# Identity products ahead of eight TensorE steps in a fused attention and two-MoE kernel

## The chip, the cores and the metric

The kernel runs on one core of one Trainium2 chip. The time is device microseconds (us) of one execution, as the median of several. Engines are named as in the profile: PE (TensorE matmul), PEld (TensorE weight load), DVE (VectorE), ACT (ScalarE), POOL (GpSimd), SP (SyncE, which issues nearly all DMAs).

## What is computed

A gated linear attention over 4 batches, 8 heads, 768 positions and head size 48; its output, as 3072 rows of 384, goes through a first MoE layer (384 to 2048 to 384, with a rational activation) and a second one (384 to 1536 to 384, gated by silu).

```python
def _attn_ref(q, k, v, alpha):
    ...
    for t in range(S):
        state = alpha[:, :, t, :, None] * state + np.einsum('bhd,bhe->bhde', k[:, :, t], v[:, :, t])
        y[:, :, t] = np.einsum('bhd,bhde->bhe', q[:, :, t], state)
def _moe_ref(x, w_in, w_out, a, b):
    h = x @ w_in
    P = a[0] + a[1] * h + a[2] * h * h + a[3] * h * h * h
    Q = 1.0 + np.abs(b[0]) * np.abs(h) + np.abs(b[1]) * h * h
    return (P / (Q + 1e-06)) @ w_out
def _moe2_ref(x, w_gate, w_val, w_out):
    g = x @ w_gate
    return (g / (1.0 + np.exp(-g)) * (x @ w_val)) @ w_out
```

## The kernel before

The attention is cut into 24 chunks of 128 positions (six to a batch). For a chunk, TensorE transposes alpha, k and q (`tr`, line 770, tiles aT, kT, qT), makes the scores (`scores`, line 821, sc), transposes the scaled k back (`back`, line 846, kn_ps), and in `values` makes the update of the state (line 865, upd), the chunk's own part of the output (line 870, yT) and the part from the state before it (line 876, yT). Between them DVE runs the two scans of the decay (lines 786 and 794, bb and cc) and scales k and q (lines 802 and 812, kt and qt), ACT copies results out of PSUM (779 al, 830 aa, 849 kn, 885 yo), and POOL masks the scores (835) and decays the state (904). The loads of a chunk are line 729 on SP's queue, into buffers that are used again: a load waits until TensorE has read the buffer. At the same time the MoE weights are split into two parts on DVE, POOL and ACT (`split_`; line 669 writes a scratch tile in a PSUM bank and line 675 reads it), and the first MoE's products (`mm1` and `mm2`, lines 955 to 957, tiles h and acc) begin as soon as 512 positions are there. The second MoE follows.

All operations are first collected in a `Plan`; each has the engine alternatives, what it depends on and the buffers that it writes. Then the table `ORDER` (lines 20 to 190) gives the order in which they are issued, written out by hand: entry x stands for operation x >> 1. Each engine runs its own operations in that order and never out of it. `Plan.order` also gives out the eight PSUM banks: the operation that opens a bank buffer takes the bank that has been free longest, and the bank goes back when the last operation on that buffer has been issued. The tile framework then adds the semaphore waits. A writer of a bank waits for the last reader of the buffer that had the bank before.

Before the attention, `keep_warm` (line 562) issues 9 products of a 128x128 identity with itself, and 20 more after the first chunk's qT; both go to bank 7, which nothing else uses at that time.

The eight operations that the change names, in the order in which TensorE reaches them (the bank is the one that the fills write, and its last reader is what `order` gives out for this table):

| operation | what it is | bank | last reader of that bank before |
|---|---|---|---|
| 90 | `tr`, aT | 5 | ACT, line 830 (aa) |
| 79 | `values` (bank of yT) | 1 | DVE, line 902 (st_c) |
| 146 | `tr`, aT | 4 | ACT, line 779 (al) |
| 135 | `values` (bank of yT) | 4 | DVE, line 675 (wout_x) |
| 161 | `values`, last chunk of a batch (yT) | 1 | DVE, line 902 (st_c) |
| 185 | `values` (bank of yT) | 4 | ACT, line 885 (yo) |
| 281 | `tr`, kT | 7 | DVE, line 902 (st_c) |
| 942 | `mm2` (bank of acc0) | 6 | DVE, line 675 (win_x) |

In `values` the products of upd come first and write another bank than yT.

Of the kernel before, what the change touches and what calls it, by code (L numbers as in the profile page):

```python
# [226 lines left out]
class Plan:  # L227
# [47 lines left out]

    def order(self, table):

        free = {c: list(range(k)) for c, k in self.classes.items()}
        todo = {}
        done = set()  # L280
        for x in table:
            i, k = x >> 1, x & 1
            _, how, deps, writes, follows = self.ops[i]
            assert i not in done and done.issuperset(deps) and done.issuperset(follows)
            done.add(i)
            for b in writes:
                if b.kind and b.ops[0] == i:
                    b.unit = free[b.cls].pop(0)
                    for j in set(b.ops):
                        todo.setdefault(j, []).append(b)  # L290
                    b.open = len(set(b.ops))
            for b in todo.get(i, ()):
                b.open -= 1
                if not b.open:
                    free[b.cls].append(b.unit)
            yield i, how[k][2]
        assert len(done) == len(self.ops)
# [160 lines left out]
def gla_moe_moe2_kernel(  # L458
# [15 lines left out]
    nc = tc.nc  # L474
# [23 lines left out]
    plan = Plan()  # L498
# [51 lines left out]
    ident = const.tile([128, 128], F32, name="ident")  # L550
# [792 lines left out]
        moe2(row, n, f0, f1, load_y(row[0], n), wg, wv, wo)  # L1343
    flag = bounds(end_a + 70.0, vs2[-1][0] - 70.0, vs2[-1][0] + 20.0)

    for x, (i, f) in enumerate(plan.order(ORDER)):
        if x == len(ORDER) - 18:
            tc.mark_branch_hint_location(
                "usual", "LikelyTaken", [mybir.EngineType.PE, mybir.EngineType.DVE, mybir.EngineType.SP])
        for b in plan.ops[i][3]:  # L1350
            if b.t is None:
                b.t = b.make()
        f()
    pb2.__exit__(None, None, None)
    pb.__exit__(None, None, None)
# [38 lines left out]
```

## Time and profile before

| | us |
|---|---|
| median of 3 runs | 989.08 |
| lowest, highest | 988.86, 990.64 |
| the profiled execution | 987.1 |
| its span, first to last instruction | 985.3 |

| engine | busy us | share | instructions |
|---|---|---|---|
| PE | 969.0 | 98% | 5355 |
| PEld | 805.6 | 82% | 5355 |
| DVE | 786.9 | 80% | 1493 |
| ACT | 588.9 | 60% | 1078 |
| POOL | 450.5 | 46% | 426 |

How to read it: the shares are means over stages that differ. In the table of 40 slices each digit is the busy share of one slice of 24.6 us in tenths, so the first four digits are the first tenth, in which attention, weight splitting and the first MoE overlap. A PE product is recorded with a modelled end, some 0.27 us after its start, while the next one can start 0.11 us after it; an idle time of PE is counted from that modelled end.

### The profile page before, as it was taken

What the parts mean: (1) busy time and instruction counts of PE and PEld (TensorE: products, weight loads), DVE (VectorE), ACT (ScalarE), POOL (GpSimd) and SP (SyncE); (2) the same over time, 40 slices, a digit from 0 to 9 for tenths busy, and PEclk for the clock granted to TensorE, in tenths of its full rate; (3) what the DMA queues carried; (4) which work ended last, traced back from release to release, by engine and by line L of the source; (5) the groups of instructions that cost most, each with busy time, mean ns of one, the idle gap of its engine ahead of it and who ended that gap; (6) DMA issues with size and microseconds to landing.
All of it is one profiled execution on the core that took longest, in us unless ns stands there. A gap on an engine that the chain in (4) does not pass through costs nothing.

```text
span 985.3 us, 15291 instructions
## 1 busy us (share of the span) xinstructions
PE 969.0 (98%) x5355; PEld 805.6 (82%) x5355; DVE 786.9 (80%) x1493; ACT 588.9 (60%) x1078; POOL 450.5 (46%) x426
## 2 busy tenths in 40 slices
PE   8899999999999999999999999999999999999997
PEld 7777888888888888888888888888888888888886
DVE  7999999999889888888898896799887767733222
ACT  4588998899999787789988675222122222212111
POOL 3368888799877676777987555000000000000000
PEclk9999999999999999999999999999999999999999
DMA  8978666531223242101221663346665545501000
GB/s 184 208 186 220 150 156 152 157 103 37 57 88 94 54 140 70 55 25 53 91 86 45 218 188 127 113 129 196 176 179 187 165 140 150 161 1 33 1 0 34
DMA packets 167137, 113.51 MB, mean 115 GB/s; under 512 B 115472, under 2 KB 140560, under 8 KB 167056
## 3 DMA queue, kind: packets, MB, share of 16 engines
q1 hardware_dynamic: 166768, 112.10, 40.7%
q8 instruction: 43, 0.70, 0.3%
q10 hardware_dynamic: 288, 0.39, 0.1%
q14 instruction: 38, 0.31, 0.1%
HBM read 95.95 MB, written 16.52 MB: 114 GB/s over the span
## 4 chain that ended last, share of the span: by engine, by line
PE 84%; DVE 8%; ACT 4%; issue 2%; POOL 1%; DMA 1%; SPq 0%; DVEq 0%; ACTq 0%; POOLq 0%
PE acc L955 6%; PE acc L956 6%; PE acc L957 6%; PE h L955 5%; PE h L957 5%; PE h L956 5%; PE pg L957 5%; PE pg L955 5%; PE pg L956 5%; PE pv L957 5%; PE pv L955 5%; PE pv L956 5%; PE po L955 4%; PE po L957 4%; PE po L956 4%
## 5 line engine op out<-in xcount | busy, mean ns | idle before, releaser
L925 POOL TENSOR_TENSOR gg<-t,gg 128x512 fp32r<-128x512 f32 x96 | 129.8, 1352 | 52.2 <-ACT gg L1014 50.9
L998 POOL TENSOR_TENSOR t<-t,t 128x512 f32<-128x512 f32 x96 | 127.7, 1332 | 29.2 <-ACT t L988 20.6
L1177 DVE TENSOR_TENSOR sg<-sg,pv 128x512 f32<-128x512 f32 (+1 forms) x73 | 49.4, 678 | 101.3 <-PE pv L957 101.0
L1179 ACT CAST pp<-sg 128x512 fp32r<-128x512 f32 (+1 forms) x73 | 44.8, 615 | 142.1 <-DVE sg L1177 126.7
L1175 ACT ACTIVATE sg<-pg 128x512 f32<-128x512 f32 (+1 forms) x73 | 43.0, 591 | 144.0 <-PE pg L957 143.8
L955 PE MATMUL h<-xt,win 128*128 128x512 f32 x288 | 114.4, 397 | 0.2 <-DVE wo_x L675 0.2
L955 PE MATMUL acc<-gg,wout 128*128 128x512 f32 x288 | 113.9, 396 | 0.5 <-DVE win_x L675 0.5
L957 PE MATMUL h<-xt,win 128*128 128x512 f32 x288 | 112.4, 390 | 0.0
L957 PE MATMUL acc<-gg,wout 128*128 128x512 f32 x288 | 112.3, 390 | 0.0
L956 PE MATMUL acc<-gg,wout 128*128 128x512 f32 x288 | 112.3, 390 | 0.0
L956 PE MATMUL h<-xt,win 128*128 128x512 f32 x288 | 112.2, 390 | 0.0
L957 PE MATMUL pg<-yy,wg 128*128 128x512 f32 x216 | 84.2, 390 | 0.0
L956 PE MATMUL pg<-yy,wg 128*128 128x512 f32 x216 | 84.2, 390 | 0.0
L955 PE MATMUL pg<-yy,wg 128*128 128x512 f32 x216 | 84.1, 389 | 0.0
L957 PE MATMUL pv<-yy,wv 128*128 128x512 f32 x216 | 84.0, 389 | 0.0
L956 PE MATMUL pv<-yy,wv 128*128 128x512 f32 x216 | 84.0, 389 | 0.0
L955 PE MATMUL pv<-yy,wv 128*128 128x512 f32 x216 | 84.0, 389 | 0.0
L1004 DVE SCALAR_TENSOR_TENSOR t<-t,h 128x512 f32<-128x512 f32 x96 | 65.4, 682 | 19.2 <-ACT h L1003 18.7
L995 ACT ACTIVATE t<-h,prm 128x512 f32<-128x512 f32 x96 | 73.8, 775 | 7.1 <-POOL gg L925 6.7
L1102 DVE TENSOR_SCALAR_CACHE_REDUCE chk_x<-chk_e 128x384 f32<-128x384 uint32 x136 | 73.6, 549 | 2.7
L1002 ACT ACTIVATE t<-t,oneps 128x512 f32<-128x512 f32 x96 | 69.5, 724 | 9.3 <-POOL t L998 8.9
L999 DVE TENSOR_TENSOR t<-t,h 128x512 f32<-128x512 f32 x96 | 65.1, 680 | 10.2 <-ACT t L995 10.0
(154 smaller groups left out, 2472.8 us busy)
## 6 DMA issues: line engine op xcount, KB each, us to landing
chk<-in_moe_w_out_dram SPq DMA_DIRECT2D x28, 384.0 KB, 3.2
yr<-y1d SPq DMA_DIRECT2D x36, 256.0 KB, 2.9
xr<-xd SPq DMA_DIRECT2D x27, 256.0 KB, 3.4
y1d<-ys SPq DMA_DIRECT2D x27, 256.0 KB, 3.2
win_st<-in_moe_w_in_dram SPq DMA_DIRECT2D x16, 384.0 KB, 4.1
wout_st<-in_moe_w_out_dram SPq DMA_DIRECT2D x16, 384.0 KB, 3.9
chk<-in_moe_w_in_dram SPq DMA_DIRECT2D x16, 384.0 KB, 3.5
nata<-in_alpha_dram SPq DMA_DIRECT2D x24, 192.0 KB, 3.6
```

What stands on the lines that cost most here:

```text
L925: return lambda: eng.tensor_tensor(out_(), in0(), in1().bitcast(F32), ALU.subtract)
L955: nc.tensor.matmul(out_, wh, xh, start=start, stop=False)
L956: nc.tensor.matmul(out_, wh, xl, start=False, stop=False)
L957: nc.tensor.matmul(out_, wl, xh, start=False, stop=stop)
L995: plan.op(v, [act(T, lambda: nc.scalar.activation(t4(), h(), AF.Identity, scale=a3, bias=a2), 2, False)], (hb,), (b4,))
L998: plan.op(v, [pool(T, lambda: nc.gpsimd.tensor_tensor(t1(), t1(), t2(), ALU.mult))], (b1, b2), (b1,))
L999: plan.op(v, [dve(T, lambda: nc.vector.tensor_tensor(t4(), t4(), h(), ALU.mult))], (b4, hb), (b4,))
L1002: plan.op(v, [act(T, lambda: nc.scalar.activation(t2(), t1(), AF.Ln, bias=oneps), 1)], (b1,), (b2,))
L1004: plan.op(v, [dve(T, lambda: nc.vector.scalar_tensor_tensor(t1(), t1(), ONE_EPS, h(), ALU.add, ALU.mult))], (b1, hb), (b1,))
L1102: [(DVE, 0.5, lambda: nc.vector.tensor_scalar(dst(), src(), bound, 0.0, op_, ALU.add, accum_out=cnt.t[:, c : c + 1]))],
L1177: plan.op(v, [(DVE, 0.07 + 0.53 * d, lambda sg=sg, z=z: nc.vector.tensor_tensor(sg.t[:, z], sg.t[:, z], pv.t[:, z], ALU.mult))], (sg, pv), ...
L1179: plan.op(v, [(ACT, 0.1 + 0.43 * d, lambda sg=sg, pp=pp, z=z: nc.scalar.copy(pp.t[:, 0, z], sg.t[:, z]))], (sg,), (pp,))
```

## The change

Eight operations get a number of products ahead of them. Just before such an operation is issued, and after its buffers have been made, the kernel issues that many transposes of the identity (128x128, the same product as in `keep_warm`) into the first 128 columns of the first bank that the operation opens. The operation's own products then overwrite the bank. `ORDER` stays as it is. `self.free` only keeps a name for the lists of free banks; nothing reads it.

```diff
     def order(self, table):
 
-        free = {c: list(range(k)) for c, k in self.classes.items()}
+        free = self.free = {c: list(range(k)) for c, k in self.classes.items()}
...
+    fills = {
+        90: 4, 79: 5, 146: 4, 135: 10, 161: 5, 185: 5, 281: 3, 942: 3,
+    }
     for x, (i, f) in enumerate(plan.order(ORDER)):
...
         for b in plan.ops[i][3]:
             if b.t is None:
                 b.t = b.make()
+        for b in plan.ops[i][3]:
+            if b.cls == "bank" and b.ops[0] == i:
+                for _ in range(fills.pop(i, 0)):
+                    nc.tensor.transpose(b.t[:, 0:128], ident, ident)
         f()
```

## Rows read from the trace of the kernel before

**Rows 1.** The page: busy tenths and granted clock in 40 slices
```profile
DVE  7999999999889888888898896799887767733222
PEclk9999999999999999999999999999999999999999
```

**Rows 2.** Busy time by stretch: length, engines (x instructions), granted clock, DMA share, GB/s
```profile
5.00:98.50 93.50, 85.55 (x899) 72.41 (x898) 90.87 (x151) 66.56 (x145) 49.95 (x56) 1.00 0.87 204
98.50:980.00 881.50, 880.10 (x4445) 730.45 (x4443) 696.07 (x1343) 521.00 (x933) 397.22 (x354) 1.00 0.36 106
```

**Rows 3.** Waits of DVE, 10 to 145 us: total, times, longest
```profile
DVE bb L786 <- ACT bC L798: 0.5, 1, 0.5
DVE wout L645 <- POOL wout_x L702: 0.4, 1, 0.4
DVE wout_x L675 <- POOL wout L645: 0.2, 1, 0.2
```

**Rows 4.** PE timeline (start, duration, what, count, [idle before]): identity products, next step
```profile
1.43 2.18 PE L562 MATMUL warm<-ident 128*128 128x128 f32 x9 [1.43 <-POOL ident masks.py:199]
6.08 2.35 PE L562 MATMUL warm<-ident 128*128 128x128 f32 x20
8.26 0.60 PE L770 MATMUL aT<-ident,nata 128*112 128x128 f32 x4
```

**Rows 5.** PE timeline: the five steps 90, 79, 146, 161 and 185
```profile
17.86 0.62 PE L770 MATMUL aT<-ident,nata 128*112 128x128 f32 x4 [0.63 <-DMA nata<-in_alpha_dram]
24.83 0.58 PE L865 MATMUL upd<-natv,kn 128*64 128x48 f32 x15 [0.87 <-ACT st_s L909]
30.61 0.62 PE L770 MATMUL aT<-ident,nata 128*112 128x128 f32 x4 [0.70 <-ACT wout L680]
44.94 1.31 PE L870 MATMUL yT<-aa,natv 128*64 128x128 f32 x16 [0.82 <-DMA natv<-in_v_dram]
51.03 0.58 PE L865 MATMUL upd<-natv,kn 128*64 128x48 f32 x15 [0.78 <-ACT al L779]
```

**Rows 6.** ACT timeline: the last reader of step 90's bank
```profile
15.88 1.07 ACT L830 COPY aa<-sc 128x512 f32<-128x512 f32 x2 [2.20 <-PE sc L821]
```

**Rows 7.** DVE timeline, 37 to 38.5 us: the bank's last reader, then qt
```profile
37.25 0.56 DVE L675 SCALAR_TENSOR_TENSOR wout_x<-wout_st,wout_e 128x384 uint32<-128x384 uint32 x1
37.72 0.68 DVE L812 TENSOR_TENSOR qt<-qT,bb 112x512 f32<-112x512 f32 x1
```

**Rows 8.** PE timeline: step 135, and a qT transpose further on
```profile
38.51 0.58 PE L865 MATMUL upd<-natv,kn 128*64 128x48 f32 x15 [1.61 <-ACT kn L849]
49.21 0.60 PE L770 MATMUL qT<-ident,natq 128*112 128x128 f32 x4
```

**Rows 9.** DVE timeline, 73 to 75.5 us: last readers of banks 7 and 6
```profile
73.91 0.34 DVE L902 TENSOR_TENSOR st_c<-upd,st_c 112x192 f32<-112x192 f32 x1
74.91 0.53 DVE L675 SCALAR_TENSOR_TENSOR win_x<-win_st,win_e 128x384 uint32<-128x384 uint32 x1
```

**Rows 10.** PE timeline: steps 281 and 942, and the next two waits behind them
```profile
74.31 0.65 PE L770 MATMUL kT<-ident,natk 128*112 128x128 f32 x4 [0.49 <-DVE st_c L902]
75.49 0.50 PE L955 MATMUL acc<-gg,wout 128*128 128x512 f32 x1 [0.54 <-DVE win_x L675]
79.74 0.60 PE L770 MATMUL qT<-ident,natq 128*112 128x128 f32 x4
80.41 0.65 PE L770 MATMUL aT<-ident,nata 128*112 128x128 f32 x4
141.00 0.61 PE L865 MATMUL upd<-natv,kn 128*64 128x48 f32 x15 [0.41 <-DVE t L1010]
```

**Rows 11.** PE, ACT and DVE timelines: where a late PE meets the next engine
```profile
50.43 0.68 DVE L812 TENSOR_TENSOR qt<-qT,bb 112x512 f32<-112x512 f32 x1
58.99 0.60 PE L770 MATMUL aT<-ident,nata 128*112 128x128 f32 x4
59.68 0.59 ACT L779 COPY al<-aT 112x512 f32<-112x512 f32 x1
```

## Prediction

> **What bounds the kernel now.** I read the page's slices first: DVE is at nine tenths from the second slice to the ninth, and the granted clock is full in all 40 slices [rows 1]. Then the busy time by stretch. From 98.5 us to 980 us TensorE is busy for 880.1 of 881.5 us, so there it sets the pace. In the first tenth it is not so: from 5 to 98.5 us TensorE is busy for 85.55 of 93.5 us and DVE for 90.87 [rows 2]. DVE's list of waits shows that it stood still for only 1.1 us between 10 and 145 us, and none of those waits is for TensorE [rows 3]. So TensorE's idle 8 us in the first tenth are, for the most part, what is left over while DVE works through its queue. The last long wait of TensorE in this region is at 141.00 us, and DVE ends it [rows 10]. A lateness of TensorE before 141 us reaches the end only if it makes DVE late, or if it is still there when that wait begins.
>
> **What a fill costs.** Twenty of the same products start at 6.08 us, and the step behind them starts at 8.26 us: 2.18 / 20 = 0.11 us each [rows 4]. The 39 products of the change are 4.3 us of TensorE. What counts is where they lie. A fill writes the bank, so it has to wait for the bank's last reader, and the operation's own products queue behind it.
>
> **Five steps where the fills lie inside the wait (90, 79, 146, 161, 185).** The waits are 0.63, 0.87, 0.70, 0.82 and 0.78 us [rows 5], and the fills take 0.44, 0.55, 0.44, 0.55 and 0.55 us. In all five, the bank's last reader ends before TensorE begins to wait. The nearest of the five is step 90: the copy of aa ends at 15.88 + 1.07 = 16.95 us [rows 6], and the wait begins at 17.86 - 0.63 = 17.23 us. What the steps wait for then (a load, kn, kt) is as late as before. I take 0. The cover is thinnest at step 146 (0.70 - 0.44 = 0.26 us) and at 185 (0.23 us).
>
> **Step 135, ten fills.** The wait is the longest, 1.61 us, from 36.90 to 38.51 us [rows 8]. But the bank of yT is the one that holds wout1's scratch tile, and its reader ends at 37.25 + 0.56 = 37.81 us [rows 7]. The fills cannot start before that; with the 0.05 us that lie between a reader's end and a product (75.44 and 75.49 at step 942 [rows 9, 10]) they start at 37.86 us and take 1.1 us. upd, whose own bank had been held until DVE's qt ended at 37.72 + 0.68 = 38.40 us [rows 7], now starts at about 39.0 us in place of 38.51: **0.5 us late**. From below 0.45 us; from above 0.6 us, if the first product after a wait and the change of bank cost some 0.1 us more.
>
> **Steps 281 and 942, three fills each.** Here the wait is for the bank itself. st_c ends at 73.91 + 0.34 = 74.25 us and kT starts at 74.31 us; win_x ends at 74.91 + 0.53 = 75.44 us and acc starts at 75.49 us [rows 9, 10]. The fills come after the wait, and the step is 0.33 us late. At 281 the next wait hides it (0.54 us in front of acc, more than 0.33). At 942 nothing is left to hide it at once: 0.33 us, and 0.4 us from above. Next, the aT at 80.41 us starts 0.67 us after a qT of four products, which take 0.44 us (79.74 to 80.18 us), so some 0.23 us of waiting for ACT absorb most of it [rows 10]. What is left, 0.1 us, goes into the 0.41 us at 141.00 us. I take 0 for both; if that cover is gone, 0.4 us.
>
> **What becomes of the 0.5 us.** Behind step 135 TensorE runs its steps in order, and what DVE needs of them has room: the tightest is the qt at 50.43 us, whose qT ends at 49.21 + 0.60 = 49.81 us, 0.62 us before [rows 8, 11]. At step 185 the 0.78 us of waiting for the load of v, less 0.55 us of fills, take up 0.23 us, so 0.27 us remain; if that load is late as well, the whole 0.5 us. The next place where another engine follows TensorE closely is ACT's copy of aT: it starts at 59.68 us, and the transposes end at 58.99 + 0.60 = 59.59 us [rows 11]. ACT is busy for 66.56 of 93.5 us of the stretch [rows 2]; how much of its idle time lies behind this point, to take a delay back, these rows do not show. So up to 0.5 us can pass through ACT into DVE's queue. I take 0.25 us, half of the 0.5. Bounds: 0 if ACT's and DVE's small gaps take it, 0.6 + 0.4 = 1.0 us if all is carried.
>
> **The clock.** The identity products ran at 2.18 / 9 = 0.24 us at 1.43 us and at 0.11 us later [rows 4]: the two levels of the clock, 1.2 and 2.4 GHz, differ by a factor of two in the rows, before and after TensorE had been busy at the start. In the waits that the change fills there is no such trace: upd takes 0.58 us after 0.87, after 1.61 and after 0.78 us of idle time alike [rows 5, 8], and the granted clock is 1.00 over the whole stretch [rows 2]. The Trainium skill, "TensorE: Matmul & The Clock Gate", section "HAM oscillation — how this bites in real kernels", says that waits for data between short bursts of products throttle the clock again, so that every burst starts cold. By that rule the fills would be worth having; by the rows there is nothing to win, and the sum goes by the rows.
>
> **The sum.** Five steps 0, step 135 +0.25, steps 281 and 942 0: +0.25 us on the profiled execution's 987.1 us. The median of the runs is 989.08 us, 1.98 us above that execution; the difference is added to the median: 989.3 us.
>
> **Rivals.** (a) *All of it is absorbed.* For: DVE's waits hold nothing from TensorE [rows 3]. Against: ACT's close step at 59.68 us. Time: 989.1 us. (b) *The clock falls in other executions than the profiled one*, and the fills keep it up. For: the runs are 1.98 us above the profiled execution, which shows no fall. Against: nothing in the rows says that they differ by the clock, and the highest run is as far from the median (1.56 us) as the profiled one nearly is. Mechanism: after a wait the attention's steps go at the half level and take twice as long, and part of it lies under DVE. It can win at most what the median is above the undisturbed execution: 987.1 to 988.2 us. This is the case in which the rule of the skill cited above holds here. (c) *Slower: DVE starts to wait for TensorE.* Place: qt at 50.43 us, with 0.62 us of room [rows 8, 11]. The lateness from step 135 is put at 0.5 to 0.6 us; from 0.62 us on each tenth of it makes DVE's queue, and so the end, a tenth later, and step 942's 0.4 us come on top because the wait at 141.00 us moves along: 0.6 + 0.4 = +1.0 us, 990.1 us. It goes over 991 only if the loads behind TensorE's steps slip as well. Against: the room is a little more than the lateness. (d) *The fills do not do what they are put there for at three of the eight steps* is not a rival but part of the forecast (135, 281, 942).
>
> **How the numbers follow.** A measurement of this kernel can tell about 0.2% from no change, that is 1.98 us: the limits are 987.1 and 991.06 us. Chances: forecast (+0.25, from 0.1 to 0.7) 0.45; (a) 0.22; (b) 0.16, a little over half of it beyond the limit; (c) 0.13, less than half of it beyond; 0.04 for what I have not seen. So faster 0.10, within 0.82, slower 0.08. The likeliest case's own range with the spread of the runs is 988.8 to 990.0 us. The range takes in half of (b) and (c)'s 990.1 us with part of the spread of the runs: 987.8 to 990.8 us.
>
> **What would show it.** In the changed kernel the first fill of step 135 should start at about 37.86 us, with some 1 us of idle time before it that DVE's wout_x ends, and upd at 39.0 us or a little later. At the five covered steps the same product should start at the same time as before, with an idle time shorter by the fills. kT should start near 74.65 us, acc near 75.85 us, and aT at 80.41 us not later than 80.55 us. The wait at 141.00 us should be there and end 0 to 0.5 us later. TensorE's instructions should be 5394 (5355 and 39), its busy time up by 3.5 to 5 us, the span by less than 1 us. The prediction is wrong if the span falls by over 1 us, if upd at step 135 starts at 38.5 us as before (then the bank was free), or if DVE's waits show one for TensorE.

## The result, and the profile after

| | before | after |
|---|---|---|
| median of 5 runs each, us | 989.08 | 994.21 |
| lowest, highest | 988.81, 990.64 | 993.45, 996.09 |
| after / before, 95% interval | | 1.0052 [1.0037, 1.0066] |
| profiled execution, its span | 987.1, 985.3 | 993.45, 991.7 |

The changed kernel is 0.5% slower; 989.3 (987.8 to 990.8) was predicted. The loss is complete early on. The windows view of after (columns as in [rows 2]) shows that the long stretch behind the first tenth has not changed. In the first tenth DVE, which sets the pace there, is busy for 86.36 us, 4.51 less than before: it stands still somewhere. And the granted clock is 0.98, with one stretch at the half level, 1.2 GHz (the third row).

```profile
5.00:98.50 93.50, 85.83 (x891) 73.58 (x891) 86.36 (x142) 60.83 (x132) 45.44 (x50) 0.98 0.80 187
98.50:980.00 881.50, 880.90 (x4463) 731.18 (x4462) 699.64 (x1347) 525.30 (x941) 403.07 (x360) 1.00 0.37 107
...
57.90:61.20 3.30, 3.30 (x20) 2.79 (x17) 2.10 (x4) 1.79 (x4) 0.95 (x2) 0.50 0.33 66
```

Where DVE stands still, and for whom TensorE waits, is in after's waits (total, times, longest): DVE's from 10 to 145 us, to be set beside [rows 3], then TensorE's from 10 to 100 us.

```profile
DVE t L999 <- ACT t L984: 4.0, 1, 4.0
DVE bb L786 <- ACT al L779: 0.5, 1, 0.5
DVE bb L786 <- ACT bC L798: 0.5, 1, 0.5
DVE wout L645 <- POOL wout_x L702: 0.4, 1, 0.4
...
PE yT L870 <- POOL aa L835: 3.4, 4, 2.9
PE upd L865 <- ACT al L779: 1.9, 1, 1.9
PE yT L1359 <- DVE wout_x L675: 1.1, 1, 1.1
```

Two waits are new and large: 2.9 us of TensorE for a mask on POOL (line 835), and 4.0 us of DVE for ACT's t (line 984), which reads TensorE's h. Both lie behind step 135, and they are one story. (The 1.9 us at upd are not part of it: they follow a long scan on DVE at 22.74 us, and e1 below waits 1.87 us there too and is not slow.) The timelines of after tell it: TensorE from step 135 on, then POOL's two masks (the second one alone in the second row), then DVE, from the qt ahead of step 135's upd on.

```profile
39.41 1.31 PE L1359 MATMUL yT<-ident 128*128 128x128 f32 x10 [1.13 <-DVE wout_x L675]
40.65 0.61 PE L865 MATMUL upd<-natv,kn 128*64 128x48 f32 x15
...
49.52 1.16 PE L821 MATMUL sc<-qt,kt 48*128 48x128 f32 x16
...
56.34 1.09 PE L870 MATMUL yT<-aa,natv 128*64 128x128 f32 x14 [2.87 <-POOL aa L835]
57.35 1.59 PE L821 MATMUL sc<-qt,kt 48*128 48x128 f32 x16
58.87 1.10 PE L770 MATMUL kT<-ident,natk 128*112 128x128 f32 x4
...
51.42 4.86 POOL L835 TENSOR_SCALAR_AFFINE_SELECT aa<-aa 128x512 f32<-128x512 f32 x2 [4.47 <-ACT aa L830]
52.01 4.27 POOL L835 TENSOR_SCALAR_AFFINE_SELECT aa<-aa 128x512 f32<-128x512 f32 x1
...
39.27 0.68 DVE L812 TENSOR_TENSOR qt<-qT,bb 112x512 f32<-112x512 f32 x1
...
51.37 0.69 DVE L802 TENSOR_TENSOR kt<-kT,cc 112x512 f32<-112x512 f32 x1
51.97 0.69 DVE L812 TENSOR_TENSOR qt<-qT,bb 112x512 f32<-112x512 f32 x1
52.57 0.56 DVE L693 TENSOR_TENSOR win_x<-win_x,win_r 128x384 f32<-128x384 f32 x1
...
55.78 0.91 DVE L645 TENSOR_TENSOR win<-win_x,win 128x384 fp32r<-128x384 f32 x1
...
64.05 0.69 DVE L999 TENSOR_TENSOR t<-t,h 128x512 f32<-128x512 f32 x1 [4.05 <-ACT t L984]
```

The same place in before (TensorE's scores, POOL's two masks, then DVE):

```profile
47.68 1.16 PE L821 MATMUL sc<-qt,kt 48*128 48x128 f32 x16
...
49.58 1.41 POOL L835 TENSOR_SCALAR_AFFINE_SELECT aa<-aa 128x512 f32<-128x512 f32 x2 [4.47 <-ACT aa L830]
...
49.83 0.69 DVE L802 TENSOR_TENSOR kt<-kT,cc 112x512 f32<-112x512 f32 x1
51.03 0.55 DVE L693 TENSOR_TENSOR win_x<-win_x,win_r 128x384 f32<-128x384 f32 x1
54.24 0.53 DVE L645 TENSOR_TENSOR win<-win_x,win 128x384 fp32r<-128x384 f32 x1
```

How to read it. DVE's kt and qt take one input from PSUM; before and after them DVE has operations with both inputs in SBUF (the scans, lines 925, 693, 689, 645). In before, the first mask had begun when kt began (49.58 against 49.83), the two ran beside kt and qt and ended at 50.99, 0.04 us before DVE's line 693. In after the first mask starts 0.05 us behind kt. The two need 1.22 us and kt and qt give 1.20 (51.37 to 52.57). So the second mask is not done when line 693 begins, and it then lasts 4.27 us instead of 0.63: it ends at 56.28, inside line 645, which is 0.38 us longer than before. TensorE waits 2.87 us for it, the clock falls to the half level behind that wait (sc 1.59 us for 1.16, kT 1.10 for 0.65), h comes late, and with h DVE's line 999.

This is theory P: the loss is a mask on POOL that came some tenths of a microsecond too late to slip past DVE. Rival Q: it is the fills' own time, in proportion to their number (the first expectations call it S). Rival T: it is DVE's scan of line 794 near 22 us, which took 1.57 us in before and 2.74 in after. A second question is what the clock costs, and a third whether the other seven steps win or lose anything.

### The profile page after: what moved, and what is told of

Its sections match the earlier page's. It is cut to its first block, busy times and chain, and to the rows that moved or that the text cites. A ratio compares the mean times of both kernels' runs of the same rounds, so it can differ in the third digit from the quotient of the medians.

```text
span 991.7 us, 15366 instructions
## 1 busy us (share of the span) xinstructions
PE 975.6 (98%) x5394; PEld 812.3 (82%) x5394; DVE 788.6 (80%) x1493; ACT 589.3 (59%) x1078; POOL 451.9 (46%) x426
## 4 chain that ended last, share of the span: by engine, by line
PE 85%; DVE 7%; ACT 4%; POOL 2%; issue 1%; DMA 1%; SPq 0%; ACTq 0%; DVEq 0%; POOLq 0%
PE acc L955 6%; PE acc L956 6%; PE acc L957 6%; PE h L955 5%; PE h L957 5%; PE h L956 5%; PE pg L956 5%; PE pg L955 5%; PE pg L957 5%; PE pv L955 5%; PE pv L956 5%; PE pv L957 5%; PE po L955 4%; PE po L956 4%; PE po L957 4%; PE sc L821 2%
## 5 line engine op out<-in xcount | busy, mean ns | idle before, releaser
L1002 ACT ACTIVATE t<-t,oneps 128x512 f32<-128x512 f32 x96 | 69.5, 724 | 9.4 <-POOL t L998 9.0
```

The lines of the kernel that those rows point to most:

```text
L1002: plan.op(v, [act(T, lambda: nc.scalar.activation(t2(), t1(), AF.Ln, bias=oneps), 1)], (b1,), (b2,))
```

## The experiments

All edits below are to the kernel before or the changed kernel; none changes what is computed. "Room" is DVE's first line 693 less the start of the second mask, from the two engines' timelines; a mask left alone takes 0.63 us.

| run | us, median (lowest to highest) | ratio to before, 95% interval | room us | second mask us | mean clock of its runs |
|---|---|---|---|---|---|
| changed kernel | 994.21 (993.45 to 996.09) | 1.0052 [1.0037, 1.0066] | 0.56 | 4.27 | 0.995 to 0.997 |
| e1_all_but_135 | 988.26 (987.96 to 989.13) | 0.9987 [0.9977, 0.9997] | 0.67 | 0.63 | 0.998 to 1.000 |
| e2_only_135 | 994.72 (993.99 to 996.63) | 1.0055 [1.0038, 1.0071] | 0.56 | 3.79 | 0.992 to 0.995 |
| e3_135_five | 988.85 (988.15 to 989.75) | 0.9994 [0.9985, 1.0004] | 0.67 | 0.63 | 0.998 to 0.999 |
| e4_pool_late | 1005.73 (1005.04 to 1006.75) | 1.0163 [1.0146, 1.0180] | 0.32 | 4.02 | 0.995 to 0.997 |
| e4b_pool_late | 994.18 (993.76 to 994.57) | 1.0053 [1.0036, 1.0070] | 0.33 | 3.56 | 0.995 to 0.996 |
| e5_dve_gap | 989.32 (988.59 to 990.25) | 1.0002 [0.9993, 1.0012] | 1.33 | 0.63 | 0.998 to 1.000 |
| e6_busy_wait | 992.32 (991.81 to 992.98) | 1.0033 [1.0020, 1.0045] | 0.56 | 4.26 | 0.998 to 0.999 |
| e7_135_eight | 988.90 (988.58 to 991.23) | 0.9997 [0.9988, 1.0006] | 0.67 | 0.63 | 0.998 to 0.999 |
| e10_135_fourteen | 991.20 (989.18 to 992.35) | 1.0015 [1.0006, 1.0025] | 0.45 | 1.96 | 0.998 to 1.000 |
| e8_before_again | 989.32 (987.01 to 991.57) | 0.9999 [0.9987, 1.0011] | 0.55 | 3.14 | 0.995 to 0.999 |
| e9_only_79 | 989.65 (987.87 to 991.61) | 1.0000 [0.9991, 1.0009] | 0.66 | 0.63 | 0.995 to 0.999 |
| e11_no_79_no_135 | 989.19 (988.60 to 991.97) | 0.9998 [0.9984, 1.0013] | 0.66 | 0.63 | 0.995 to 0.999 |
| e12_all_but_135_again | 988.80 (987.88 to 989.71) | 0.9988 [0.9974, 1.0001] | 0.67 | 0.63 | 0.998 to 0.999 |

The chips differ a little (before had a median of 989.33 to 989.86 beside these runs), so ratios are what is compared. In before's own profile the room is 0.67 us and the mask 0.63. Room and mask are those of the one profiled execution of each kernel; the times are those of all its runs.

### Which of the eight steps costs the time

**e1_all_but_135, e2_only_135, e3_135_five.** The fills of seven steps, of step 135 alone, and of all with half as many at 135:

```diff
-        90: 4, 79: 5, 146: 4, 135: 10, 161: 5, 185: 5, 281: 3, 942: 3,
+        90: 4, 79: 5, 146: 4, 161: 5, 185: 5, 281: 3, 942: 3,  # e1
+        135: 10,  # e2
+        90: 4, 79: 5, 146: 4, 135: 5, 161: 5, 185: 5, 281: 3, 942: 3,  # e3
```

> Theory P (POOL's mask): the ten fills of step 135 make TensorE late against DVE, the scores of the chunk behind come late, and POOL's second mask of that chunk (0.63 us before, 4.27 us in the changed kernel) runs into DVE operations with two inputs in SBUF. Without those ten fills the mask should end in under 1 us again, TensorE's wait of 2.87 us at yT and the half-rate stretch behind it should be gone: 989 to 990 us. Rival S (sum of small delays: every fill costs, wherever it lies): 29 of 39 fills stay, so about 993 us. Rival T (the slow scan at 22.7 us and the later start, which have nothing to do with step 135): 992 to 994 us.

> Only the ten fills of step 135. Theory P: the whole loss, 993 to 995 us, with the mask at 4 us or more and a stretch of the clock at half. Rival S: ten of 39 fills, so about 990.4 us. Rival T: about 989 us.

> All eight steps, but five fills at step 135. The bank is free at 37.8 us and upd cannot start before 38.5 us, so five fills (0.55 us and 0.1 us) end just in time. Theory P: TensorE is not late, 989 to 990 us. Rival S: 34 of 39 fills, about 993.5 us. A rival within P, that it is the number of instructions at this place and not the lateness: half of the loss, 991.5 us.

Step 135 alone carries the whole loss (1.0055), the other seven carry none of it (0.9987), and five fills in place of ten at 135 cost nothing that can be told from before. Five products less are 0.55 us of TensorE, and they change the time by 5 us: a cost of this kind is not the products' own time. Rival T falls with e1: its scan of line 794 takes 2.74 us too (at 22.42 us), and its profiled execution is 988.09 us.

### Is it the mask, and not TensorE's order?

**e4_pool_late, e4b_pool_late.** The kernel before without one identity product; only POOL's second mask is put off, by three small writes on POOL ahead of it.

```diff
+    late = const.tile([128, 1], F32, name="late")  # e4
...
+        if i == 182:
+            for _ in range(3):
+                nc.gpsimd.memset(late, 1.0)  # e4
+                nc.gpsimd.memset(oneps, ONE_EPS)  # e4b, in place of it
         f()
```

> The kernel before, with no fills, and three memsets of one column on POOL (0.09 us each) ahead of the one mask that took 4.27 us in the changed kernel. Theory P: the mask then ends 0.2 to 0.3 us later than at 50.99 us, after the start of DVE's addition of two SBUF tiles at 51.03 us, and is held up by some 3.5 us as in the changed kernel: 992 to 995 us. Rivals S and T: nothing of TensorE is changed, 989 to 989.5 us.

> The kernel before, without any identity product; POOL alone gets three more writes of a one-column constant it already has, just ahead of its mask of operation 182 (line 835, the second of the pair at about 50 us), so that this mask starts some 0.3 to 1 us later against DVE. Theory P (a mask that is late enough to meet DVE's chain of additions, lines 693, 689, 786, is held up, TensorE waits some 3 us for it and its clock falls): the pair of masks goes from 1.41 to 4 us or more, TensorE's yT waits over 2 us for the mask near 52 us, 992 to 996 us although TensorE has no product more. Rival Q (the loss comes from the fills' own time and their order on TensorE): the pair of masks stays below 2.5 us, 988.5 to 990 us. No growth of DVE's lag is expected behind 580 us, because no tile is added.

e4 took longer than theory P allows. Its mask took 4.02 us, and DVE ran 6.6 to 7.4 us behind before's profile from 66 to 584 us (e4b: 6.9 to 7.4), as theory P says, but a second lag grew behind 584 us: the second MoE's products took 395 to 396 ns on the mean in place of 389 to 390. The new tile is 4 bytes a partition and may move the addresses of what lies behind it; whether that is the cause was not tried. e4b has no new tile and no such lag: 994.18 us. Its POOL and TensorE timelines:

```profile
51.53 0.41 POOL L1355 MEMSET oneps<- 128x1 f32 x3
51.88 3.56 POOL L835 TENSOR_SCALAR_AFFINE_SELECT aa<-aa 128x512 f32<-128x512 f32 x1
...
55.49 1.54 PE L870 MATMUL yT<-aa,natv 128*64 128x128 f32 x14 [2.82 <-POOL aa L835]
56.97 2.08 PE L821 MATMUL sc<-qt,kt 48*128 48x128 f32 x16
```

Without a fill, three writes of 0.41 us together ahead of one mask cost as much as the whole change. Rival Q can't give that.

**e5_dve_gap.** The reverse: the changed kernel with its 39 fills, and DVE's line 693 put off by three writes of its own, so that the late mask can end first.

```diff
+        spare.append(cnt)
...
+    spare = []
...
+        if i == 685:
+            for _ in range(3):
+                nc.vector.memset(spare[0].t, 1.0)
         f()
```

> The changed kernel with its 39 products, and three more small writes on DVE (136 columns each, some 0.1 to 0.25 us each) ahead of its addition of operation 685 (line 693, the first of the chain at about 52.6 us), so that the late mask on POOL may end before the chain begins. Theory P: the mask pair falls from 4.86 to below 2.5 us, TensorE's wait of 2.87 us at yT goes below 1.2 us, the granted clock does not fall at 57 to 61 us; DVE pays some 0.5 us once: 989 to 990.5 us. Rival Q (the fills' own time): 994 to 995 us, the loss stays and 0.5 us come on top.

POOL and DVE of e5 (the tile that is written has 160 columns, not 136):

```profile
51.07 1.22 POOL L835 TENSOR_SCALAR_AFFINE_SELECT aa<-aa 128x512 f32<-128x512 f32 x2 [4.47 <-ACT aa L830]
...
52.30 0.78 DVE L1364 MEMSET cnt<- 128x160 f32 x3
52.99 0.49 DVE L693 TENSOR_TENSOR win_x<-win_x,win_r 128x384 f32<-128x384 f32 x1
```

The masks take 1.22 us, no wait over 1 us is left at yT, and 0.78 us of useless work on the engine that sets the pace makes the kernel 5 us faster than the changed one. Theory P stands from both sides: the mask is late without a fill and the loss is there, the fills are there with the mask free and the loss is gone. What no run varies is the inputs of the DVE operations. That it is their two inputs in SBUF which hold the mask is read from the rows: it runs in 0.63 us beside kt and qt, and it was held beside the chain that begins with line 693.

### What of it is the clock

**e6_busy_wait.** The mask stays late, but TensorE is kept busy inside the 2.87 us wait, by products in `values` between upd and yT of that chunk:

```diff
+            if m == 6:
+                for _ in range(28):
+                    nc.tensor.transpose(yT.t[:, 0:128], ident, ident)
```

> The changed kernel, and 28 more identity products in the chunk whose yT waits 2.87 us for the mask, between its upd and its yT, that is inside that wait. The mask stays late; only TensorE does not stand still. If part of the loss is the clock that falls behind that wait (0.50 from 57.9 to 61.2 us), the granted clock stays over 0.9 there, DVE's wait for t (4.05 us at 64 us) becomes 2.2 to 3 us, and the time is 992 to 993 us. If the clock only follows and costs nothing, 994 to 994.7 us as the changed kernel.

The windows view and DVE's timeline of e6 (its lines are three further on: L1002 is line 999):

```profile
57.00:61.20 4.20, 4.20 (x34) 3.56 (x33) 2.47 (x5) 2.09 (x5) 1.54 (x3) 1.00 0.55 115
...
62.20 0.69 DVE L1002 TENSOR_TENSOR t<-t,h 128x512 f32<-128x512 f32 x1 [2.57 <-ACT t L987]
```

The clock holds at 2.4 GHz, DVE's wait is 2.57 us for 4.05, and the time is 992.32. So of the loss against the kernels with a free mask (988.9), some 3.4 us are the mask and 1.9 us the clock that falls behind the wait for it (1.6 us between the two profiled spans, 991.7 and 990.1; DVE's wait is 1.5 us shorter).

### A threshold or a price for each product?

**e7_135_eight, e10_135_fourteen.** Eight and fourteen fills at 135 in place of ten, all else as in the change.

> The changed kernel with eight products at step 135 in place of ten: TensorE is 0.22 us less late there. Theory P (a threshold: the mask has to end before DVE's line 693 begins, and was some 0.1 us too late): the mask pair is below 1.6 us, no wait over 1 us at yT, 988.3 to 989.3 us. Rival Q (a cost in proportion to the products): between five (988.85) and ten (994.2 to 994.7), about 992 us.

> The changed kernel with fourteen products at step 135 in place of ten: TensorE is 0.44 us later still. Theory P (a threshold, past which the mask ends with DVE's chain, however late it came): the mask pair still ends near 56.3 us on DVE's time, 993.5 to 995.5 us, within 1 us of the changed kernel. Rival Q (in proportion; ten cost some 5 us): 996 to 997 us.

Eight cost nothing (0.9997, second mask 0.63 us): two products, 0.22 us of TensorE, decide about 5 us. Fourteen, where I had expected the same loss as with ten and rival Q more, cost less: 991.20, outside both. POOL and DVE of the profiled execution (989.18, the lowest of its ten):

```profile
51.40 1.96 POOL L835 TENSOR_SCALAR_AFFINE_SELECT aa<-aa 128x512 f32<-128x512 f32 x1
...
50.65 0.69 DVE L802 TENSOR_TENSOR kt<-kT,cc 112x512 f32<-112x512 f32 x1 [0.37 <-PE kn_ps L846]
51.85 0.55 DVE L693 TENSOR_TENSOR win_x<-win_x,win_r 128x384 f32<-128x384 f32 x1
52.79 1.66 DVE L786 TENSOR_TENSOR_SCAN bb<-al,seed_f 112x516 f32<-112x516 f32 x1
```

Now TensorE is so late that DVE itself waits 0.37 us for kn_ps, and the mask comes through at the scan, which pays 0.43 us (1.66 for 1.23), where in after it comes through only at line 645, four operations later. Over the table, a room of 0.66 us or more leaves the mask at 0.63 us; from 0.56 us down it takes 1.96 to 4.27 us, and the length does not follow the room. So there is a threshold, and behind it the hold ends at one of DVE's operations, but which one isn't settled here. This execution is also of another kind than after's: its scan of line 794 takes 1.57 us (at 22.29), as in before's profile, where after's takes 2.74, so DVE comes to kt earlier (it starts at 50.65 us, after 0.37 us of waiting, against 51.37). The other nine runs of e10 are 1.6 to 3.2 us longer than the profiled one; how long the mask is held in them, no trace shows, and why fourteen cost less than ten stays open.

### What the other seven steps do

**e8_before_again.** The kernel before, unedited.

> The kernel before without an edit, for its profile and its spread. If the profiled execution of before (scan of line 794 at 22 us 1.57 us, clock at 1.00 throughout) is one of several kinds, this one may show the scan at 2.7 us and a clock of about a half at 26 to 29 us as the kernel with the ten fills alone does; 988.5 to 990 us. If the clock falls there only where something was added, the scan is 1.57 us or the clock stays over 0.9 with a scan of 2.7 us; 988.5 to 990 us as well.

It has the same median, and its profiled execution (991.2 us) isn't like the one shown before the prediction. DVE's timeline, POOL's and TensorE's, then the windows view, then POOL's again:

```profile
22.66 2.73 DVE L794 TENSOR_TENSOR_SCAN cc<-al,seed_r 112x516 f32<-112x516 f32 x1
...
23.09 1.22 POOL L835 TENSOR_SCALAR_AFFINE_SELECT aa<-aa 128x512 f32<-128x512 f32 x2
...
26.30 0.58 PE L865 MATMUL upd<-natv,kn 128*64 128x48 f32 x15 [2.48 <-ACT al L779]
...
26.00:30.00 4.00, 3.71 (x40) 3.33 (x40) 3.97 (x10) 0.29 (x2) 0.25 (x1) 0.65 0.61 157
...
52.01 3.73 POOL L835 TENSOR_SCALAR_AFFINE_SELECT aa<-aa 128x512 f32<-128x512 f32 x2 [4.78 <-ACT aa L830]
```

The same two rows in the first profile of before:

```profile
22.36 1.57 DVE L794 TENSOR_TENSOR_SCAN cc<-al,seed_r 112x516 f32<-112x516 f32 x1
...
22.82 2.13 POOL L835 TENSOR_SCALAR_AFFINE_SELECT aa<-aa 128x512 f32<-128x512 f32 x2
```

The scan of line 794 takes 2.73 us in e8, with both masks done inside it in 1.22 us; in the first profile it was the masks that took longer (2.13) and the scan less (1.57). The first profile is the rare kind: of the 15 profiled executions, 13 have the long scan (2.73 or 2.74 us), and only before's and e10's have the short one. Behind the long scan TensorE waits 2.48 us at upd of step 79 (0.87 in [rows 5]); the clock falls behind that wait; TensorE is late, and the second mask takes 3.14 us. So the kernel before meets the same threshold by itself in at least this execution. (The fall alone does not do it: e11 below has the fall and a mask of 0.63 us.) Its runs spread from 987.0 to 991.6 us here, and from 986.6 to 995.8 us over all that were taken beside the experiments: the longest are as long as those of the changed kernel. None of those has a trace.

**e9_only_79, e11_no_79_no_135, e12_all_but_135_again.** Step 79's fills alone; six steps without 79 and 135; e1 once more.

```diff
+        79: 5,  # e9
+        90: 4, 146: 4, 161: 5, 185: 5, 281: 3, 942: 3,  # e11
+        90: 4, 79: 5, 146: 4, 161: 5, 185: 5, 281: 3, 942: 3,  # e12
```

> The kernel before with the five products of step 79 alone. Theory C (the wait of 1.9 to 2.5 us at upd near 24 us lets the clock fall in some executions, and the products shorten it): no execution shows a fall at 26 to 30 us, the runs lie within about 1.2 us as those of the kernel with all fills but step 135's (987.96 to 989.13), median 988.0 to 988.6 us. Rival (the gain of that kernel comes from other steps, or there is none): median 989.0 to 989.6 us with runs from 988 to 991.5 us, as before.

> The changed kernel without the products of steps 79 and 135 (six steps are left, 24 products). Theory C1 (the products of step 79 are needed to hold the clock, though with them alone it wasn't held): executions with a mean clock of 0.995 to 0.997 appear, the runs spread over 3 us or more, median 989.2 to 990 us. Rival C2 (the other six steps hold the clock, step 79 has no part in it): all executions at 0.998 or more, the runs within 2 us, median 988.1 to 989.0 us.

> The changed kernel without the products of step 135, once more, beside the kernel before on another chip and in more rounds. If the seven steps keep the clock and step 135 alone does the harm: all executions at 0.998 or more, 988.0 to 989.0 us, 0.05 to 0.2% under the kernel before. If the gain measured earlier was that chip's or chance: ratio 0.9995 to 1.0005.

Theory C fell as I had put it: step 79's fills alone neither gain (1.0000) nor narrow the spread. But the clock speaks for C1 against C2: without them e11 has executions at 0.995 again and a spread of 3.4 us, and its profiled execution shows the fall at that very place, in TensorE's timeline and the windows (0.91 from 26 to 28 us, 0.50 from 28 to 34):

```profile
26.55 0.58 PE L865 MATMUL upd<-natv,kn 128*64 128x48 f32 x15 [1.94 <-ACT al L779]
...
30.30 2.08 PE L821 MATMUL sc<-qt,kt 48*128 48x128 f32 x16
...
30.00:34.00 4.00, 4.00 (x27) 3.52 (x27) 2.23 (x3) 1.17 (x3) 1.32 (x2) 0.50 0.96 215
```

So step 79's fills seem to be needed and don't do it alone. This rests on the clock: 5 of e11's 12 runs lie below 0.998 and none of e12's 12; the ratios of the two (0.9998 and 0.9988) overlap in their intervals. Every run of the kernels that have the fills of all seven other steps and no long idle wait for the mask (e1, e12, e3, e7, e5, e6, e10) has a mean clock of 0.998 or more. Before, e8, e9 and e11 have runs at 0.995. Which of the other steps loses the clock in e9 stays open, since none of its slowest runs has a trace. The gain is small: 0.9987 [0.9977, 0.9997] and, in the repeat, 0.9988 [0.9974, 1.0001], which just takes in no gain. Both were taken on the same chip, so e12 is not the test on another chip that its expectation speaks of. The kernel without step 135's fills has the lowest ratio of those that were run, not clear of those with five and eight fills there (0.9994 and 0.9997).

## Why the prediction was wrong, step by step

**Right.** A fill costs 0.11 us, and the five covered steps cost nothing: e1 has their fills and is at 0.9987. Step 135 went as described: the fills wait 1.13 us for wout_x, and upd, which began 0.79 us behind DVE's qt (38.51 less 37.72 [rows 7, 8]), begins 1.38 us behind it (40.65 less 39.27): 0.59 us late, inside 0.45 to 0.6, at its upper end. The two steps whose wait is the bank itself are late by 0.38 us (fills at 80.73, kT at 81.11) and 0.30 us (81.92, acc at 82.22), for 0.33; the wait that was at 141.00 us is at 147.37 and has 0.43 us as before (0.41), so the 0.4 us of that cover were not needed. TensorE's instructions are 5394.

**Right in the time, not in the reason.** The waits of [rows 5] belong to one execution. In after TensorE has no wait left at 146 and 185. At 185, where the prediction had 0.23 us of cover, upd begins 0.29 us behind the end of ACT's kn (52.28 and 52.57 us); in e2 and e9, without fills there, it is 0.05 and 0.06 us. So the fills at 185 make their step some 0.24 us late. That this is free was luck, as far as the argument goes: e1 has the same (0.30 us behind kn) and loses nothing. Two readings were off without effect: [rows 1] has DVE at nine tenths to the tenth slice, not the ninth, and the row of step 185 names ACT's al as what came last, not the load of v.

**The step that failed: "What becomes of the 0.5 us".** It went from TensorE to the engines that wait for TensorE's results, looked for the least time between an end and the next start, and found 0.62 us at qt. That was a list of semaphore waits. The tightest place was one step further and no semaphore waited there: sc on TensorE (47.68 before, 49.52 after: 1.84 later, while DVE's kt was 1.54 later; so 0.30 of the 0.59 us were still there), ACT's aa, POOL's mask, which in before had ended 0.04 us ahead of DVE's next operation with two inputs in SBUF. The room was 0.04 us at the end of the masks, or about 0.25 us at their start (49.58 against 49.83), not 0.62. And the bound from above, 1.0 us, took a lateness as something that is at most handed on; here 0.3 us became 4 us of DVE standing still, because a 0.63 us operation turned into one of 4.27 and the clock fell behind it. The rows of DVE and POOL around 50 us would have shown how narrowly the masks fit beside kt and qt, and those at 22.82 us that another pair of masks had taken 2.13 us beside a scan in the very same trace.

The Trainium skill, "SBUF — State Buffer", section "Who interferes with whom", says that a DVE instruction with two SBUF inputs contends with a GpSimd instruction that reads SBUF, and that the order of issue decides who blocks. The trace agrees with the first and not with the second as it stands: the mask began at 52.01 us, line 693 at 52.57, and it was the mask that was held, for over 3 us. Had the mask, as the first one, not been held, it would have ended at 52.64 us and DVE would have lost 0.07 us, by an estimate from these rows; the time would then have been near that of e7.

**Rival (c)** (chance 0.13; slower beyond the limit had 0.08 in all) had the right sign and the wrong place and price: DVE did come to wait for TensorE, at t (4.05 us), through h and ACT, not at qt. In e10 it waited for kn_ps as well (0.37 us), close to the mechanism named.

**The clock: the step took one execution for all.** [rows 2] showed 1.00 throughout, and the sum took nothing. Behind longer waits the clock does fall (0.65 in e8, 0.50 in after and e11). In after it cost 1.9 us more than in e6, and rival (b), that other executions than the profiled one lose the clock and the fills keep it, is what the mean clocks of before, e1, e11 and e12 show. It put the time at 987.1 to 988.2 us; measured were 988.26 and 988.80, so the gain is smaller than it said and in the repeat not clear of none. The rule of the Trainium skill cited in the prediction, that waits for data between bursts throttle the clock again, is borne out by these rows, but not at the waits of under 1 us in [rows 5]: the falls shown stand behind waits of 1.94 (e11), 2.48 (e8) and 2.87 us (after). And e4b waits 2.48 us at the same place as e8 and keeps its clock (1.00 from 26 to 30 us), so a long wait does not always lose it.

**The base of the sum.** The profiled execution of before, 1.98 us under the median, was the rare kind with the short scan and a free mask. e1's profiled execution, with the long scan and a free mask, spans 986.4 us, 1.1 us more than before's 985.3, so about half of the 1.98 us goes with the scan (2.74 less 1.57 is 1.17), and e8 shows the long scan without the change. The difference was added as a constant; in part at least it is made of waits, clock falls and masks that the change acts on.

## What to carry over

Before work is added to one engine, follow its lateness past the first waiting engine, and look there at what runs beside what, not only at who waits for whom: an operation on POOL that ends just ahead of DVE work on two SBUF inputs has the room of that gap, whatever the semaphores say. Ten fills at step 135 were worse than none and eight were free: what a late step costs is set by what it meets further on, not by the length of the fills. Where runs spread by 0.3% and the profile is from their lower edge, take a second profile before reasoning from "no fall".

## What the runs showed of the hardware that I had not expected

- POOL's mask of 128x512 takes 0.63 us alone and beside DVE operations with one PSUM input, and 1.96 to 4.27 us, in seven profiled executions, where a chain of DVE operations with two SBUF inputs began before it ended. DVE pays little there: 0.38 us at line 645, 0.43 us at a scan.
- A near tie can go either way, and then it can be DVE that pays: POOL's decay of the state starts 0.02 to 0.03 us ahead of DVE's scan of line 794 in before and in e8 alike (22.34 and 22.36, 22.63 and 22.66), and the scan takes 1.57 us in the one and 2.73 in the other. What decides it is not shown.
- A new 4-byte tile (e4) came with products of the second MoE that took 395 to 396 ns on the mean in place of 389 to 390, some 12 us over the kernel; the cause was not tried.
